# Feed-forward cut into 12 segments of 384 tokens, u stationary in its second layer, and one buffer each for raw q/k, v and shifts

## The chip, the cores and the metric

The kernel runs on one core of a Trainium2 chip. The metric is the device time of one execution in microseconds (us). Of the kernel before, three runs took 761.41, 757.99 and 758.09 us, so the median is 758.09 us. The engines are named as in the profile: PE is TensorE (the matrix engine; PEld is its weight loading), DVE is VectorE, ACT is ScalarE, POOL is GpSimd, and SP is the engine whose queue issues all the DMAs of this kernel.

## The reference

Eight sequences of 576 tokens go through causal attention with 8 heads of 64 and a bias from running sums, and then through a gated feed-forward of width 1024 with a convolution of three taps along the tokens.

```python
B, H, S, D = 8, 8, 576, 64
cum = np.cumsum(np.maximum(s, 0.0), axis=-1)
scores = np.matmul(q, k.transpose(0, 1, 3, 2)) / np.sqrt(D)
scores = scores + np.minimum(-(cum[..., :, None] - cum[..., None, :]), 0.0)
attn = softmax(np.where(causal, -1e9, scores))
x = np.matmul(attn, v).transpose(0, 2, 1, 3).reshape(B, S, 512)
h = np.maximum(x @ w_in, 0.0)                    # w_in: 512 x 1024
conv = sum(conv_w[k] * hp[:, k:k + S] for k in range(3))   # hp: h with a zero row at both ends
out = (h * sigmoid(conv)) @ w_out                # w_out: 1024 x 512, out: 8 x 576 x 512
```

## The kernel before, in words

**Work.** Two heads make a pair, four pairs a sequence, and there are 32 pairs. A pair's attention on PE is: shift products `sh` (scores whose maxima DVE takes, L1098 and L1130), a transpose of the maxima (L1156), the scores `sc` in 4 parts (L1209), column sums (L1324) and the product with v (L1267). ACT turns scores into weights (L1224). From pair 8 on, `ORDER` ties `sh` of the next pair, `sc` of this one and the sums and the product of the one before into one block on PE, which this text calls a burst.

**Feed-forward.** Each sequence is cut into two halves of 288 tokens. Half `hf` of sequence `b` runs its first layer once per 128 of the 1024 hidden channels (`moe_h`): 12 matmuls on a 290-column tile of x (288 and a neighbour at each side; 4 blocks of 128 inputs, times 3 products of high and low parts), then ReLU (L1437), the centre tap (L1442), two side taps (L1455), the sigmoid (L1467), the product with h (L1473), and the split of the result into a high part (L1481) and a low part (L1485), two channel blocks at a time. The second layer (`moe_o`, L1513) keeps a 128 by 128 block of w_out in the array and streams 288 columns of u past it; its result has the output channels on the partitions, so the kernel stores `outT` and the host transposes it. There are 1536 matmuls of 290 columns and 1536 of 288.

**What sets the order.** Every piece is a task of a planner (`Sched.play`), which walks forward with assumed durations and gives each engine the ready task with the smallest due number (`DUE`). The recorded order is then the program. The planner also holds the pools of buffers: a task that allocates waits until a slot is free. `BUFS` gives 2 raw q/k tiles, 2 tiles of q and k parts, 3 `ek`, 3 `eq` (the shifts), 5 u tiles and 2 output tiles; v has 2, and x has 5 and 7 tiles for the two halves. Until 112 us of its own plan the planner fills waits of PE with dummy matmuls (L1560).

Of the kernel before, what the change touches and what calls it, by code (L numbers as in the profile page):

```python
# [1628 lines left out]
```

## Time and profile before

| | before |
|---|---|
| median of three runs | 758.09 us |
| span of the profiled execution | 757.9 us |
| PE busy | 739.8 us, 98% |
| DVE, ACT, POOL busy | 490.4, 458.0, 381.5 us |
| matmuls of the feed-forward | 1536 of 290 columns, 1536 of 288 |
| last matmul ends, last ACT copy starts | 754.79, 754.85 us |

The profiled execution's span of 757.9 us stands 0.2 us below the median of the runs, so a sum made on the span is carried over by adding 0.2. A busy PE isn't PE at its peak: matmuls overlap, and a row's mean duration is longer than the distance from one matmul to the next. For the distance, the starts of a timeline or the pieces of the chain of waits are read.

### The profile page before, as it was taken

Reading aid. Unit: us, or ns where it says so; the run is one execution under the profiler, and the core shown is the slowest. Engines: PE = TensorE matmul, PEld = TensorE weight load, DVE = VectorE, ACT = ScalarE, POOL = GpSimd, SP = SyncE. Lnnn points to the kernel's source line nnn. Section 1 sums busy time; section 2 is a strip of 40 time slices with the busy share of each in tenths; the row PEclk is TensorE's granted clock in tenths of the full one; section 3 lists DMA queues with packets and bytes.
Section 4 is the critical chain, followed back from the end, with each engine's and each line's share of the span. In section 5 each row is a group of like instructions: output and inputs, shape, how many; then the busy total and the mean of one; then the engine's idle time right before and its main releaser. Section 6 shows DMA issues by size and latency. Waiting matters only on the chain.

```text
span 757.9 us, 20341 instructions
## 1 busy us (share of the span) xinstructions
PE 739.8 (98%) x7822; PEld 664.0 (88%) x7822; DVE 490.4 (65%) x1390; ACT 458.0 (60%) x1070; POOL 381.5 (50%) x459
## 2 busy tenths in 40 slices
PE   9999999999999999999999999999999999999998
PEld 7666779978989989898999899898998889899998
DVE  8676997545766657586664776666675866633632
ACT  5467887445765656555755756566575556653633
POOL 5257456524866444654755755654545446521211
PEclk9999999999999999999999999999999999999999
DMA  7877662223333231424333242333324131111000
GB/s 213 261 230 211 222 215 66 91 83 115 108 114 108 81 119 58 122 91 117 99 89 116 77 130 68 116 111 116 100 52 147 55 95 33 36 34 48 16 32 32
DMA packets 55159, 80.18 MB, mean 106 GB/s; under 512 B 14041, under 2 KB 34841, under 8 KB 55001
## 3 DMA queue, kind: packets, MB, share of 16 engines
q1 hardware_dynamic: 55061, 78.87, 33.9%
q8 instruction: 61, 1.00, 0.6%
q14 instruction: 37, 0.30, 0.1%
HBM read 67.48 MB, written 10.98 MB: 104 GB/s over the span
## 4 chain that ended last, share of the span: by engine, by line
PE 87%; DMA 5%; DVE 4%; issue 2%; ACT 1%; SPq 0%; POOL 0%; DVEq 0%; ACTq 0%
PE ps L1424 27%; PE ps L1513 27%; PE ps L1209 13%; PE pv L1267 11%; PE ps L1098 4%; PE ps L1324 3%; DVE ps L1130 2%; DMA bb<-cum_d 2%; DMA w<-w_in 1%; DMA eq<-rt 1%; DVE r L1130 1%; DMA rb<-ri_d 1%; DMA ri_d<-ri 1%; DMA v<-vp 0%; PE ps L1156 0%
## 5 line engine op out<-in xcount | busy, mean ns | idle before, releaser
L1513 PE MATMUL ps<-u,wo 128*128 128x288 f32 x1536 | 220.5, 298 | 0.9 <-ACT ob L1530 0.5
L1424 PE MATMUL ps<-x,wi 128*128 128x290 f32 x1536 | 218.8, 298 | 1.2 <-ACT ob L1530 1.2
L1424 PEld LDWEIGHTS ps<-x,wi 128*128 128x128 f32 x1536 | 209.8, 190 | 2.8 <-ACT ob L1530 1.4
L1513 PEld LDWEIGHTS ps<-u,wo 128*128 128x128 f32 x1536 | 207.2, 188 | 4.3 <-ACT ob L1530 0.7
L1224 ACT ACTIVATE pt<-ps,bias_sb 128x288 f32<-128x288 f32 (+4 forms) x384 | 155.2, 478 | 74.5 <-PE ps L1209 73.2
L1455 DVE SCALAR_TENSOR_TENSOR ct<-ps,cw_sb,ct 128x287 f32<-128x287 f32 (+1 forms) x256 | 129.2, 513 | 73.0 <-ACT ct L1442 70.7
L1485 POOL TENSOR_TENSOR u<-ct,u 128x576 fp32r<-128x576 f32 x64 | 92.0, 1439 | 161.4 <-ACT u L1481 123.5
L1130 DVE CUSTOM_DVE_ANT_0 ps<-ps,bb 128x64 f32<-128x64 f32 (+4 forms) x320 | 133.7, 452 | 53.8 <-PE ps L1098 27.4
L1209 PE MATMUL ps<-s 64*128 64x288 f32 (+4 forms) x1152 | 119.8, 306 | 5.8 <-DVE r L1130 4.5
L1209 PEld LDWEIGHTS ps<-s 64*128 64x128 f32 x1152 | 95.6, 185 | 16.8 <-DVE r L1130 11.5
L1071 POOL TENSOR_SCALAR_AFFINE_SELECT bb<-bb 128x256 f32<-128x256 f32 (+1 forms) x125 | 53.2, 433 | 105.8 <-DVE r L1130 86.6
L1242 POOL TENSOR_SCALAR_AFFINE_SELECT pt<-pt 128x256 f32<-128x256 f32 (+1 forms) x160 | 69.4, 445 | 65.5 <-ACT pt L1224 55.5
L1267 PE MATMUL pv<-pt,v 128*32 128x448 f32 (+4 forms) x1536 | 94.5, 389 | 2.3 <-DVE rb L1374 2.3
L1437 ACT ACTIVATE ps<-ps 128x289 f32<-128x289 f32 x128 | 50.8, 396 | 71.2 <-PE ps L1424 68.9
L1032 POOL TENSOR_TENSOR s<-raw,s 128x1152 fp32r<-128x1152 f32 x30 | 88.2, 2940 | 9.6 <-ACT s L1028 6.8
L1267 PEld LDWEIGHTS pv<-pt,v 128*32 128x32 f32 x1536 | 57.7, 110 | 35.4 <-issue 25.7
L1467 ACT ACTIVATE ct<-ct 128x288 f32<-128x288 f32 x128 | 56.2, 440 | 33.1 <-DVE ct L1455 32.6
L1473 DVE TENSOR_TENSOR ct<-ct,ps 128x288 f32<-128x288 f32 x128 | 57.1, 448 | 22.3 <-ACT ct L1467 21.2
L1442 ACT ACTIVATE ct<-ps,cw_sb 128x288 f32<-128x288 f32 x128 | 63.8, 498 | 5.3 <-ACT ps L1437 0.4
L1209 PE MATMUL ps<-eq,ek 64*128 64x288 f32 (+4 forms) x384 | 64.5, 300 | 1.2 <-DMA eq<-rt 1.2
L1098 PE MATMUL ps<-s 64*128 64x288 f32 (+4 forms) x384 | 58.7, 340 | 0.4 <-DVE r L1130 0.2
L1130 DVE DVE_READ_ACCUMULATOR2_ANT r<- 128x1 f32 x384 | 53.8, 140 | 0.0
(89 smaller groups left out, 687.8 us busy)
## 6 DMA issues: line engine op xcount, KB each, us to landing
raw<-qk SPq DMA_DIRECT2D x32, 576.0 KB
bb<-cum_d SPq DMA_DIRECT2D x32, 576.0 KB
v<-vp SPq DMA_DIRECT2D x32, 320.0 KB
rb<-ri_d SPq DMA_DIRECT2D x64, 144.0 KB
outT<-ob SPq DMA_DIRECT2D x64, 144.0 KB
w<-w_out SPq DMA_DIRECT2D x8, 512.0 KB
w<-w_in SPq DMA_DIRECT2D x8, 512.0 KB
rows_d<-bx SPq DMA_DIRECT2D x1, 1215.0 KB
```

The source lines that it names most:

```text
L1032: tt_on(e)(st[:, 0:2, :], R_t[raw.slot], st[:, 2:4, :].bitcast(F32), op=ALU.subtract)
L1098: nc.tensor.matmul(dst[j], l, S_t[sb.slot][r, 2, c0:c1], start=True, stop=not (early and diagonal(tau, c1)),)
L1130: nc.vector.tensor_tensor_reduce(out=src, in0=src, in1=in1, scale=1.0, scalar=acc if c0 else -3.0e38, op0=ALU.add, op1=ALU.max, accum_out=acc,
L1209: nc.tensor.matmul(dst[j], l, m, start=(k == 0), stop=(k == 3))
L1224: nc.scalar.activation(PT_t[pts[j].slot][0:jt, O_T[t] + c0 : O_T[t] + c1], bank(pb, o, o + c1 - c0)[0:jt], AF.Sigmoid, bias=bias_sb[0:jt, ...
L1242: nc.gpsimd.affine_select(out=reg, in_=reg, pattern=[[0, 2], [1, min(P, W_T[t])]], compare_op=ALU.is_ge, fill=0.0, base=0, channel_multipl ...
L1267: nc.tensor.matmul(pvt[gs, o0 : o0 + c1 - c0], vt[0:jt, t, gs], PT_t[pts[g // 2].slot][0:jt, O_T[t] + c0 : O_T[t] + c1], start=(t == 0), s ...
L1424: nc.tensor.matmul(bank(hb, 0, XW), l, r, start=(k == 0), stop=(k == len(seq) - 1))
L1442: nc.scalar.activation(C_t[ct.slot][:, i, :], bank(hb, 2 * hf, 2 * hf + HS), AF.Copy, scale=cw_sb[:, 3 * f + 1 : 3 * f + 2],)
L1455: nc.vector.scalar_tensor_tensor(cc[:, lo:hi], bank(hb, hf + sh + lo, hf + sh + hi), cw_sb[:, 3 * f + k : 3 * f + k + 1], cc[:, lo:hi], op ...
L1485: tt_on(e)(uu[:, 1], C_t[ct.slot], uu[:, 0].bitcast(F32), op=ALU.subtract)
L1513: nc.tensor.matmul(bank(pb, 0, HS), l, r, start=(fp == 0 and k == 0), stop=(fp == NF // 2 - 1 and k == len(seq) - 1),)
```

## The change

The tokens of two sequences in a row (1152) are cut into 3 segments of 384, the middle one made of the last 192 tokens of one and the first 192 of the next (each with its own neighbours: 2 times 194 columns). The first layer streams 386 or 388 columns. The second layer keeps a 128-token block of u in the array and streams 512 columns of w_out, so its result has the tokens on the partitions and the rows go out as the output has them. x is copied in two pieces per pair (`rb` gets a zero column at both ends). The first two parts of `sh` are cut at 448 and 576 columns instead of 288 and 576. raw, v and eq have one buffer each, and a second one for pairs 1, 3 and 5 (v: 1 and 3) that is given back before the u tiles are opened; `ek` has 2. The table `DUE` has new numbers.

```diff
-BUFS = 2, 2, 3, 3, 4, 5, 3, 2
+BUFS = 1, 2, 2, 1, 4, 5, 3, 2
-NX = (5, 7)
+NX = 11
+    SEG = 3 * P
+    CUT = S - SEG
+    PER = 2 * S // SEG
+    NSEG = B * S // SEG
+    FIRST = {"raw": (1, 3, 5), "v": (1, 3), "eq": (1, 3, 5)}
...
-    SH_PARTS = [[(L, 0, HS)], [(L, HS, S)], [(3, 0, P * 4 - PAD), (0, 0, P - PAD)],
+    SH_PARTS = [[(L, 0, S - P)], [(L, S - P, S)], [(3, 0, P * 4 - PAD), (0, 0, P - PAD)],
...
+        if b % 2 == 0:
+            pieces = [(seg, 0, 0, SEG + 2), (seg + 1, 0, SEG, CUT + 2)]
+        else:
+            pieces = [(seg + 1, CUT + 2, 0, CUT + 2), (seg + 2, 0, CUT, SEG + 2)]
...
-    def moe_h(b, hf, fp):
+    def moe_h(g, fp):
+        G = 2 if g % PER == 1 else 1
+        W = SEG // G
...
                     nc.tensor.matmul(
-                        bank(hb, 0, XW), l, r, start=(k == 0), stop=(k == len(seq) - 1)
+                        bank(hb, 0, G * (W + 2)), l, r, start=(k == 0), stop=(k == len(seq) - 1)
                     )
...
-                    seq += [(wo[:, 0, f, ms], uu[:, 0, i]), (wo[:, 1, f, ms], uu[:, 0, i]),
-                            (wo[:, 0, f, ms], uu[:, 1, i])]
+                    seq += [(uu[:, 0, i, ms], wo[:, 0, f, :]), (uu[:, 0, i, ms], wo[:, 1, f, :]),
+                            (uu[:, 1, i, ms], wo[:, 0, f, :])]
                 for k, (l, r) in enumerate(seq):
                     nc.tensor.matmul(
-                        bank(pb, 0, HS), l, r, start=(fp == 0 and k == 0),
+                        bank(pb, 0, DM), l, r, start=(fp == 0 and k == 0),
...
-                out[b, ms, hf * HS : (hf + 1) * HS], moe_tiles["ob"][ob.slot]
+                out.rearrange("b s d -> (b s) d")[r0 : r0 + P, :], moe_tiles["ob"][ob.slot]
```

On PE, behind the attention of the last pair, the program before has 14 groups of 6 matmuls of the second layer (two output tiles and most of two more) and then the first layer of the last half; these are its rows from the last product with v on:

```order
L1267 MATMUL pv<-pt,v_94 32x64 x4
L1513 MATMUL ps_65<-u_1744,wo 128x288 x6
L1513 MATMUL ps_65<-u_1743,wo 128x288 x6
L1513 MATMUL ps_65<-u_1745,wo 128x288 x6
L1513 MATMUL ps_65<-u_1741,wo 128x288 x6
L1513 MATMUL ps_66<-u_1744,wo 128x288 x6
```

The program now has, at the same place, 10 groups of 512 columns with w_out and u in each other's role, and behind them the first layer of segment 10:

```order
L1372 MATMUL pv<-pt,v_90 32x64 x4
L1622 MATMUL ps_65<-wo,u_1776 128x512 x6
L1622 MATMUL ps_65<-wo,u_1780 128x512 x6
L1622 MATMUL ps_65<-wo,u_1777 128x512 x6
L1622 MATMUL ps_65<-wo,u_1778 128x512 x6
L1622 MATMUL ps_66<-wo,u_1776 128x512 x6
L1622 MATMUL ps_66<-wo,u_1780 128x512 x6
L1622 MATMUL ps_66<-wo,u_1777 128x512 x6
L1622 MATMUL ps_66<-wo,u_1778 128x512 x6
L1622 MATMUL ps_65<-wo,u_1776 128x512 x6
L1622 MATMUL ps_65<-wo,u_1780 128x512 x6
L1541 MATMUL ps_66<-x,wi 128x388 x12
```

Over the whole program 256 such groups of 6 became 144, and 128 first-layer groups of 12 became 96 (64 of 386 columns, 32 of 388).

On SP, in the middle of the program, one round of a pair's DMAs before reads as follows; `eq` is the shift tile, `raw` the q and k of a later pair, and `rc`, `ri_d` and `rb` the way of the column sums:

```order
L1172 DMA eq_88<-rt_101 2x5x128
L1538 DMA outT<-ob_1746 128x288
L1346 DMA rc<-rs 64x1x9 x2
L1021 DMA v_95<-vp 128x640
L1356 DMA ri_d<-ri 128x9
L1366 DMA rb<-ri_d 64x576
L1366 DMA rb<-ri_d 64x4x144
L1042 DMA ek_85<-rows_d 9x576 x2
L1060 DMA bb_92<-cum_d 128x2x576
L1172 DMA eq_88<-rt_101 2x5x128
```

The same round in the program now is:

```order
L1277 DMA eq_86<-rt_96 2x5x128
L1110 DMA raw_81<-qk 128x1152
L1451 DMA rc<-rs 64x1x9 x2
L1117 DMA v_90<-vp 128x640
L1461 DMA ri_d<-ri 128x9
L1471 DMA rb<-ri_d 64x576
L1471 DMA rb<-ri_d 64x4x144
L1145 DMA ek_84<-rows_d 9x576 x2
L1110 DMA raw_81<-qk 128x1152
L1163 DMA bb_88<-cum_d 128x2x576
L1277 DMA eq_86<-rt_96 2x5x128
```

Before, 25 of the last 26 shift DMAs already went to the one tile `eq_88`; raw went to `raw_81` 14 times and to `raw_82` 12 times in the last 26. In the short gap between two bursts that comes before the product with v of pair 11, PE now has five groups of the second layer and the transpose of the maxima as the second row:

```order
L1622 MATMUL ps_65<-wo,u_1777 128x512 x6
L1261 MATMUL ps_66<-ident,r_94 128x128
L1622 MATMUL ps_65<-wo,u_1776 128x512 x6
L1622 MATMUL ps_65<-wo,u_1778 128x512 x6
L1622 MATMUL ps_65<-wo,u_1779 128x512 x6
L1622 MATMUL ps_69<-wo,u_1779 128x512 x6
L1203 MATMUL ps_65<-s_83 128x448
```

Before, the gap in front of pair 14's product has eight groups of the second layer (48 matmuls) and one of the first, and the transpose as the fourth row; the rows there are:

```order
L1513 MATMUL ps_67<-u_1741,wo 128x288 x6
L1513 MATMUL ps_67<-u_1744,wo 128x288 x6
L1424 MATMUL ps_68<-x,wi 128x290 x12
L1156 MATMUL ps_65<-ident,r_99 128x128
L1513 MATMUL ps_67<-u_1745,wo 128x288 x6
L1513 MATMUL ps_66<-u_1741,wo 128x288 x6
L1513 MATMUL ps_66<-u_1744,wo 128x288 x6
L1513 MATMUL ps_66<-u_1745,wo 128x288 x6
L1513 MATMUL ps_66<-u_1743,wo 128x288 x6
L1513 MATMUL ps_67<-u_1743,wo 128x288 x6
L1098 MATMUL ps_65<-s_83 128x288
```

Behind the last first-layer groups of segment 10 there stand four groups of the second layer and one of the first before a group that reads the u they lead to; in segment 11, the last one, six groups of the second layer stand there. The dummy matmuls of the start number 195 before and 217 now; all of them stand ahead of the first row of the feed-forward in both programs, and so do the products with v of pairs 0 to 4.

## Rows read from the trace of the kernel before

**Rows 1.** The page: busy time and share of each engine, and the granted clock in 40 slices.

```profile
PE 739.8 (98%) x7822; PEld 664.0 (88%) x7822; DVE 490.4 (65%) x1390; ACT 458.0 (60%) x1070; POOL 381.5 (50%) x459
...
PEclk9999999999999999999999999999999999999999
```

**Rows 2.** The chain of waits of the whole program: share of the span by line.

```profile
by line: PE ps L1424 27.4%; PE ps L1513 27.2%; PE ps L1209 13.2%; PE pv L1267 10.6%; PE ps L1098 4.2%; PE ps L1324 3.4%; DVE ps L1130 2.1%; issue 1.8%; DMA bb<-cum_d 1.5%; DMA w<-w_in 1.4%; DMA eq<-rt 0.7%; DVE r L1130 0.6%; DMA rb<-ri_d 0.
```

**Rows 3.** Busy time in two stretches: length, then each engine, clock, DMA share, GB/s.

```profile
0.00:101.00 101.00, 93.88 (x1164) 68.11 (x1168) 79.17 (x246) 67.71 (x144) 53.63 (x77) 1.00 0.76 231
166.00:687.00 521.00, 513.97 (x5479) 472.18 (x5481) 341.18 (x976) 317.10 (x757) 280.91 (x336) 1.00 0.30 92
```

**Rows 4.** Pieces of the chain at the end: start us, us, line, matmuls.

```profile
701.20 9.69 PE ps L1424 x72
...
742.08 12.71 PE ps L1513 x96
```

**Rows 5.** Timeline of PE in a burst: start us, us, line, tiles, shape, count.

```profile
316.85 0.56 PE L1209 MATMUL ps<-s 64*128 64x288 f32 x6
317.25 0.29 PE L1209 MATMUL ps<-eq,ek 64*128 64x288 f32 x2
317.38 0.39 PE L1098 MATMUL ps<-s 64*128 64x448 f32 x4
...
318.80 0.77 PE L1209 MATMUL ps<-s 64*128 64x448 f32 x6
319.40 0.37 PE L1209 MATMUL ps<-eq,ek 64*128 64x448 f32 x2
319.61 0.42 PE L1209 MATMUL ps<-s 64*128 64x64 f32 x6
...
320.29 0.62 PE L1209 MATMUL ps<-s 64*128 64x320 f32 x6
320.75 0.31 PE L1209 MATMUL ps<-eq,ek 64*128 64x320 f32 x2
320.89 0.47 PE L1209 MATMUL ps<-s 64*128 64x192 f32 x6
```

**Rows 6.** Timeline of PE at the start: dummy matmuls.

```profile
10.76 6.28 PE L1560 MATMUL pv<-still 64*128 64x256 bf16 x56
```

**Rows 7.** Waits of PE: line <- releaser: us in total, times, longest.

```profile
PE ps L1424 <- ACT ob L1530: 1.2, 1, 1.2
PE ps L1209 <- DMA eq<-rt: 1.2, 1, 1.2
```

**Rows 8.** Timeline of PE: the first matmuls behind one burst.

```profile
304.48 1.73 PE L1513 MATMUL ps<-u,wo 128*128 128x288 f32 x11
```

**Rows 9.** Timeline of the SP queue around the same place.

```profile
299.87 0.34 SPq L1021 DMA_DIRECT2D v<-vp  x1
...
308.91 0.61 SPq L1172 DMA_DIRECT2D eq<-rt  x1
309.97 0.36 SPq L1016 DMA_DIRECT2D raw<-qk  x1
```

**Rows 10.** Timeline of POOL: the low part of q and k.

```profile
307.28 2.66 POOL L1032 TENSOR_TENSOR s<-raw,s 128x1152 fp32r<-128x1152 f32 x1
```

**Rows 11.** Pieces of the chain in the first 120 us.

```profile
84.90 2.90 PE pv L1267 x48
...
98.48 2.83 PE pv L1267 x48
101.32 5.04 PE ps L1424 x36
```

**Rows 12.** Timeline of ACT at the end: ReLU of the last channels, last copy.

```profile
742.11 0.40 ACT L1437 ACTIVATE ps<-ps 128x289 f32<-128x289 f32 x1 [0.29 <-PE ps L1424]
...
754.85 0.40 ACT L1530 COPY ob<-ps 128x288 f32<-128x288 f32 x1 [0.40 <-PE ps L1513]
```

**Rows 13.** Timeline of POOL at the end: the last low part of u.

```profile
746.61 1.43 POOL L1485 TENSOR_TENSOR u<-ct,u 128x576 fp32r<-128x576 f32 x1 [1.93 <-ACT u L1481]
```

More of the change, by code (lines that the diff above doesn't have):

```diff
@@ L506, in play @@
                     lock[e] = needs
-                post(now + max(dur - HIDE[e], min(dur, 0.05)), "free", t)
+                hide = o[4] if len(o) > 4 else HIDE[e]
+                post(now + max(dur - hide, min(dur, 0.05)), "free", t)
                 if e == "SP":
@@ L613 @@
     base_sb = const.tile([2 * NT, NP, 2], F32, name="base_sb")
-    V_t = [const.tile([P, NT, P], F32, name=f"v{i}") for i in range(2)]
+    V_t = [const.tile([P, NT, P], F32, name="v0")]
     PT_a = const.tile([P, NPT, O_T[-1] + W_T[-1]], F32, name="pt")
     PT_t = [PT_a[:, i, :] for i in range(NPT)]
-    X_t = const.tile([P, sum(NX), 2, XW], F32R, name="x")
-    rb_t = const.tile([P, S], F32, name="rb")
+    X_t = const.tile([P, NX, 2, XW], F32R, name="x")
+    rb_t = const.tile([P, S + 2], F32, name="rb")
     R8_t = [const.tile([P, P], F32, name=f"r{i}") for i in range(2)]
@@ L623 @@
     rc_t, ri_t = (const.tile([P, RW], F32, name=n) for n in ("rc", "ri"))
-    H_a = const.tile([P, NHT, 2 * XW], F32, name="ht")
-    H_t = [H_a[:, i, :].rearrange("p (a c) -> p a c", a=2) for i in range(NHT)]
-    C_t = [const.tile([P, 2, HS], F32, name=f"ct{i}") for i in range(NHT)]
+    H_a = const.tile([P, NHT, S - P], F32, name="ht")
+    H_t = [H_a[:, i, :] for i in range(NHT)]
+    C_t = [const.tile([P, 2, SEG], F32, name=f"ct{i}") for i in range(NHT)]
     WPC = 256
@@ L655, in open_moe @@
         stage_stack.close()
+        early_stack.close()
         mp = ctx.enter_context(tc.tile_pool(name="mp", bufs=1))
-        moe_tiles["u"] = [mp.tile([P, 2, 2, HS], F32R, name=f"u{i}") for i in range(NRING)]
-        moe_tiles["ob"] = [mp.tile([P, HS], F32, name=f"ob{i}") for i in range(NOB)]
+        moe_tiles["u"] = [mp.tile([P, 2, 2, SEG], F32R, name=f"u{i}") for i in range(NRING)]
+        moe_tiles["ob"] = [mp.tile([P, DM], F32, name=f"ob{i}") for i in range(NOB)]
     sch = Sched()
@@ L675, in buf, with first, place @@
         return Buf(pools[name], n)
+    def first(name, p):
+        return buf(name + "_e" if p in FIRST[name] else name)
+    def place(b):
+        return 1 if b.pool in (pools["raw_e"], pools["v_e"], pools["eq_e"]) else b.slot
     def psb():
@@ L749 @@
     t_s = add("s", [("SP", 0.4)], [], -200, lambda e: nc.sync.dma_start(s_sb, s), nbytes=147456)
-    t_masks = add("masks", [("POOL", 4.4)], [], -190, c_masks)
+    t_masks = add("masks", [("POOL", 4.4, True)], [], -190, c_masks)
     t_pads = [
-        add(f"pads{i}", [("DVE", 2.0) if i == 0 else ("POOL", 2.2)], [], -189 + i,
+        add(f"pads{i}", [("DVE", 2.0) if i == 0 else ("POOL", 2.1, True)], [], -189 + i,
             c_pads(i))
@@ L755 @@
     ]
-    t_ident = add("ident", [("POOL", 2.9)], [], -189.5, c_ident)
+    t_ident = add("ident", [("POOL", 2.8, True)], [], -189.5, c_ident)
     t_ind = [
-        add(f"ind{i}", [("ACT", 0.72)], [t_masks], -187 + i, c_ind(EQ_t[i])) for i in range(NEQ)
+        add(f"ind{i}", [("ACT", 0.72)], [t_masks], -187 + i, c_ind(EQ_t[i])) for i in range(len(EQ_t))
     ]
@@ L767, in cum_chain @@
         )
-    t_cum8 = add("cum", [("DVE", 2.0, True)], [t_s, t_ones], -170, cum_chain)
+    t_cum8 = add("cum", [("DVE", 2.1, True)], [t_s, t_ones], -170, cum_chain)
     def grid_chain(e):
@@ L778, in grid_chain @@
         nc.vector.memset(ncr[:, 0:1], 0.0)
-    t_cum = add("grid", [("DVE", 1.5, True)], [t_cum8], -169, grid_chain)
+    t_cum = add("grid", [("DVE", 1.9, True)], [t_cum8], -169, grid_chain)
     def base_in(e):
@@ L1027, in hi @@
             st = S_t[sb.slot]
-            copy_on(e)(st[:, 2:4, :], R_t[raw.slot])
+            copy_on(e)(st[:, 2:4, :], R_t[place(raw)])
         def lo(e):
             st = S_t[sb.slot]
-            tt_on(e)(st[:, 0:2, :], R_t[raw.slot], st[:, 2:4, :].bitcast(F32), op=ALU.subtract)
+            tt_on(e)(st[:, 0:2, :], R_t[place(raw)], st[:, 2:4, :].bitcast(F32), op=ALU.subtract)
+        if p in FIRST["raw"]:
+            early_left.append(f"lo{p}")
+        if p in FIRST["v"]:
+            early_left.append(f"pv{p}")
+        if p in FIRST["eq"]:
+            early_left.append(f"sc{p}.{len(SC_PARTS) - 1}")
         t_hi = add(f"hi{p}", [("ACT", c_act(2 * S)), ("DVE", c_cp(2 * S), True, 2.0)], [t_load],
                    a_sh - HIA, hi, alloc=[sb], uses=[raw])
-        t_lo = add(f"lo{p}", [("POOL", c_pool(2 * S), True), ("DVE", c_tt(2 * S), True, 4.0 if p >= B0 else LO1)],
+        in_order("hi", t_hi)
+        t_lo = add(f"lo{p}", [("POOL", c_pool(2 * S) + 0.08, True), ("DVE", c_tt(2 * S), True, 4.0 if p >= B0 else LO1)],
                    [t_hi], A - LOA, lo, uses=[raw, sb])
@@ L1147, in pair @@
                         f"mx{p}.{j}.{tau}.{c0}",
-                        [("DVE", 0.19 + w / 0.96e3)],
+                        [("DVE", 0.235 + (c1 - c0) / 0.96e3, False, 0.0, 0.16 if c0 == 0 else 0.1)],
                         need, a_sh + 0.1 * i, sh_max, uses=[pbs[j], r8, bb],
@@ L1461, in moe_h @@
             for k in (0, 2):
-                t_k = add(f"ta{b}.{hf}.{f}.{k}", [("DVE", 0.53)], [t_k], tg + 0.1,
+                t_k = add(f"ta{g}.{f}.{k}", [("DVE", 0.63)], [t_k], tg + 0.1,
                           lambda e, k=k, tap=tap: tap(e, k), uses=[hb, ct])
@@ L1467, in gate @@
                 nc.scalar.activation(cc, cc, AF.Sigmoid)
-            t_g = add(f"ga{b}.{hf}.{f}", [("ACT", c_act(HS))], [t_k], tg + 0.2, gate, uses=[ct])
+            t_g = add(f"ga{g}.{f}", [("ACT", c_act(SEG))], [t_k], tg + 0.2, gate, uses=[ct])
             def mul(e, i=i, hb=hb):
-                cc = C_t[ct.slot][:, i, :]
-                nc.vector.tensor_tensor(cc, cc, bank(hb, 2 * hf, 2 * hf + HS), op=ALU.mult)
-            products.append(add(f"mu{b}.{hf}.{f}", [("DVE", c_tt(HS))], [t_g], tg + 0.2, mul,
+                nc.vector.tensor_tensor(mid(i), mid(i), seen(hb, 1), op=ALU.mult)
+            products.append(add(f"mu{g}.{f}", [("DVE", c_tt(SEG))], [t_g], tg + 0.2, mul,
                                 uses=[hb, ct]))
-        tg = h_tag(b, hf, 2 * fp + 1) + 0.2
+        tg = h_tag(g, 2 * fp + 1) + 0.2
         def u_hi(e):
@@ L1485, in u_lo, with moe_o @@
             tt_on(e)(uu[:, 1], C_t[ct.slot], uu[:, 0].bitcast(F32), op=ALU.subtract)
-        t_uh = add(f"uh{b}.{hf}.{fp}",
-                   [("DVE", c_cp(2 * HS), True, 1.0), ("ACT", c_act(2 * HS))],
-                   products + ([*t_wi.values(), *t_wo.values()] if b == 0 else []), tg, u_hi,
+        t_uh = add(f"uh{g}.{fp}",
+                   [("DVE", c_cp(2 * SEG), True, 1.0), ("ACT", c_act(2 * SEG))],
+                   products + ([*t_wi.values(), *t_wo.values(), *early_done] if g == 0 else []), tg, u_hi,
                    uses=[ct, u])
-        gate_done[b, hf, fp] = add(
-            f"ul{b}.{hf}.{fp}",
-            [("POOL", c_pool(2 * HS), True), ("DVE", c_tt(2 * HS), True, 3.0)], [t_uh], tg, u_lo,
+        gate_done[g, fp] = add(
+            f"ul{g}.{fp}",
+            [("POOL", c_pool(2 * SEG), True), ("DVE", c_tt(2 * SEG), True, 3.0)], [t_uh], tg, u_lo,
             uses=[ct, u],
         )
-        u_bufs[b, hf, fp] = u
-    def moe_o(b, hf, m):
+        u_bufs[g, fp] = u
+    def moe_o(g, m):
         ob, pb = buf("ob"), psb()
-        last = (b, hf) == (B - 1, 1)
-        tg = h_tag(b, hf, NF) + HT / NF * (1.0 + OTF * m)
+        last = g == NSEG - 1
+        tg = h_tag(g, NF) + HT / NF * (1.0 + OTF * m)
         ms = slice(m * P, (m + 1) * P)
@@ L1549 @@
             sch.need(d, sch.tasks[i])
-    for b in range(B):
-        for hf in range(2):
-            for fp in range(NF // 2):
-                moe_h(b, hf, fp)
-        for hf in range(2):
-            for m in range(NM):
-                moe_o(b, hf, m)
+    early_done = [t for t in sch.tasks if t.name in early_left]
+    for g in range(NSEG):
+        for fp in range(NF // 2):
+            moe_h(g, fp)
+        for m in range(SEG // P):
+            moe_o(g, m)
     def stay_awake(slot, mode, lane):
@@ L1627 @@
     r = _run(nc, [arrays], core_ids=[0])
-    return _np.ascontiguousarray(r.results[0]["outT"].transpose(0, 2, 1))
+    return _np.ascontiguousarray(r.results[0]["out"])
```

145 lines of the change are left out of this document (78 added, 67 removed), and 540 rows, old and new, of the table DUE.

## The prediction

> **What bounds the kernel now.** The page comes first: PE is busy for 739.8 of 757.9 us, no other engine for more than 65%, and its granted clock stays in the top tenth in every slice, that is at the 2.4 GHz level [rows 1]. So only what PE does, or waits for, can move the time. The chain of waits says of what this time is made: the two layers of the feed-forward hold 27.4 and 27.2% of the span, together 54.6% of 757.9, which is 413.8 us [rows 2]. Then the stretches: in the first 101 us, before the feed-forward begins, PE's busy time has dummies in it and DMA stands at 0.76 of its capacity; from 166 to 687 us PE is busy for 513.97 of 521 us, with DVE at 341 and ACT at 317 [rows 3]. In that long stretch an engine other than PE has a third of its time to spare.
>
> **The matmuls of the feed-forward.** The columns stay the same to the last one: 1536 times 290 is 768 times 386 plus 384 times 388, and 1536 times 288 is 864 times 512. What goes is 1056 of 3072 matmuls. So the gain is whatever a matmul costs beside its columns. Before, 72 matmuls of 290 columns take 9.69 us and 96 of 288 take 12.71 us, which is 134.6 and 132.4 ns each [rows 4]; in all 206.7 + 203.4 = 410.1 us. The trace has no full-height matmul of 386 or 512 columns. The nearest rows are the scores, where two matmuls of half height run side by side. Eight of them (four side-by-side steps) with 288 columns take from 316.85 to 317.38, 132.5 ns a step, just as the full-height ones; with 320 columns from 320.29 to 320.89, 150 ns; with 448 from 318.80 to 319.61, 202.5 ns [rows 5]. From 288 to 448 that is 0.4375 ns a column, from 320 to 448 it is 0.41. I take the middle, 0.425, since 448 is the row nearest to 512. Then 386 columns cost 134.6 + 96 x 0.425 = 175.4 ns, 388 cost 176.2, and 512 cost 132.4 + 224 x 0.425 = 227.6. The sum is 134.7 + 67.7 + 196.6 = 399.0 us, 11.1 less than now. The ends: with 0.41 the gain is 15.6 us; if all of a matmul's time went with its columns it is nothing.
>
> A rule speaks against this term. The rows show 132.4 ns for 288 columns, 12.4 ns above 288 columns at 2.4 GHz (120.0). The Trainium skill (TensorE: Matmul & The Clock Gate, section "Back-to-back issue gap") gives the gap as N/2.4 ns plus only 2.5 ns for a warm matmul; the trace doesn't agree with the sum of the two, as it has about 10 ns more, and if those 10 ns go with the columns, then 1056 matmuls give back only 2.6 us. That is the first rival below.
>
> **Edges.** The chain has 413.8 us for the two layers, the dense matmuls make 410.1. The 3.7 us between them are lost where one group ends and something else begins, over 384 groups; 240 are left, so 1.4 us go (0 to 3.7).
>
> **Dummies and the start.** One dummy takes 6.28 / 56 us, 0.112 us [rows 6], and 22 more stand before the first layer's first row: 2.5 us if each is a wait that PE wouldn't have had. They only fill waits and none is on the way of data, the weights and the first pairs' DMAs are the same ones in nearly the same order, and one `ek` tile less is cleared. So the bounds are -1 and +2.5, and I take +1.2.
>
> **Output tiles.** One wait of 1.2 us on a copy of the output [rows 7] should go: with two output tiles, PE came back to one after two times 24 matmuls of 132 ns (6.4 us), now after two times 24 of 228 ns (10.9 us). I take -1.2 (0 to -1.2).
>
> **One buffer each.** I cost this at nothing. Shifts: the DMA into `eq` is issued at 308.91, 4.4 us after the burst that reads the tile ended at 304.48 [rows 8, 9], and 25 of the last 26 pairs already use one and the same tile. It waits for the maxima, not for a buffer; of PE's waits only one of 1.2 us is for that DMA [rows 7]. v: its DMA is issued at 299.87, inside the burst [rows 9], as soon as the product with the old v is over, and is used in the next burst, some 14 us later. Raw: its DMA is issued at 309.97, right at the end of the low part of q and k at 307.28 + 2.66 = 309.94 [rows 9, 10]; so it waits for that operation already. With one tile the next load always waits so; behind it on SP stand only stores and the next pair's sums. If one of the three came late by 1 us a pair, 24 bursts would lose 24 us, but the shortest gap between bursts in which this has to fit is five groups, 30 x 0.228 = 6.8 us, where before it was eight groups of 132 ns matmuls, 6.4 us (at pair 30), and the waits of PE show none there.
>
> **Off the path.** x is copied in 64 pieces instead of 32, which costs ACT, DVE and POOL some 32 short operations each; the gate's operations get a third longer and a quarter fewer. All of it lies beside PE in the long stretch, in DVE's and ACT's spare third.
>
> **The end.** The last copy (0.40 us for 288 columns, at 754.85 [rows 12]) gets 512 columns, 0.6 us, and the last store 256 KB instead of 144. What lies behind the copy now is 757.9 - 755.25 = 2.65 us; I add 0.4 for it. Together +0.6 (0 to 2.3, if both went with their size).
>
> **The sum.** 757.9 - 11.1 - 1.4 + 1.2 - 1.2 + 0.6 = 746.0, and 0.2 for the median's distance from the profiled span: 746.2, or 746 us.
>
> **Rivals.**
>
> *The time goes with the columns.* For it: 10 of the 12.4 ns may be a slower stream, as the step from 288 to 448 gives 0.4375 ns a column, above the 0.4167 of 2.4 GHz. Against it: the step from 320 to 448 is 0.41. Then the first term is 0, and the time is 746.2 + 11.1 = 757.3; with the 0.4375 it is 7.3 us and the time 750, so this rival holds from 752 up. By the rule of the page named above it would be 754.7. Chance 0.16.
>
> *Fixed cost and the full clock.* The other end: slope 0.41, all edges gone: 746.2 - 4.5 - 2.3 = 739.4. Chance 0.12 for 736 to 742.
>
> *A starved start.* The second sequence's attention now has only segment 0 to be mixed with. Until the product with v of pair 8, 51 us of feed-forward were done before, and 35 us now; pairs 5 to 8 must follow each other faster by 16 us in all. Without any feed-forward the products of two pairs come 98.48 - 84.90 = 13.6 us apart [rows 11], while the weights are being unpacked. The attention of such a pair is some 11 us of PE, and the feed-forward in front of products 5 to 8 is 10.6, 4.2, 13.1 and 7.6 us: the tightest distance is 15.2 us, above 13.6. If the pairs can't go faster than the 25 us of before, up to 16 us come back: 750 to 762. Chance 0.07.
>
> *The gate is late (slower).* A segment's last hidden channels go through ReLU, taps, sigmoid, product and split before the second layer may use them. At the end of the kernel before, that way takes from 742.08, where the last first-layer matmul gives way [rows 4, 12], to 746.61 + 1.43 = 748.04 [rows 13]: 5.96 us. With 384 columns it is between 5.96 and 4/3 of it, 7.9 us. PE has in hand for it, by the order, 24 x 0.228 + 12 x 0.175 = 7.6 us in segment 10 and 36 x 0.228 = 8.2 in segment 11. If POOL or DVE make the way longer than 9 us, each of 12 segments waits over 1.3 us, and the kernel is slower than before; at 9.1 us it is 746 + 12 x 1.5 = 764. Chance 0.08.
>
> **How the numbers follow.** A measurement tells a change from none at about 0.5%, 3.8 us: faster is under 754.3, slower over 761.9. The forecast has 0.57, for 742 to 751, its own range. Faster is the forecast, the full clock, and half each of the starved start and a fifth of the first rival: 0.57 + 0.12 + 0.035 + 0.03, about 0.76. Slower is the gate, 0.08, with next to nothing from the starved start. The rest, 0.16, is no change. The range 739 to 757 leaves out some 0.05 below and 0.14 above.
>
> **What would show it.** In the profile after: second-layer matmuls 228 ns apart in the last stretch (235 would be the first rival, 225 the second), first-layer ones 175; the two layers at about 401 us in the chain; the first of them at 101 to 104 us; no wait of PE on the raw, v or eq DMAs; the product with v of pair 8 some 10 to 16 us earlier than now. A wait of PE on u, or on the gate's engines, in every segment would make me wrong.

## The result, and the profile after

The changed kernel takes 753.85 us, the median of 7 runs (752.56 to 754.83); the kernel before, beside it on the same chip, 760.89 (757.99 to 764.55). The ratio is 0.991, with a 95% interval of 0.988 to 0.994. So it is faster, but by about three fifths of what was forecast: the profiled spans went from 757.9 to 750.6 us, 7.3 less, where the sum of the terms was 11.9 less. 746 us was not reached, and 753.85 lies above the forecast's own range of 742 to 751.

The page and the head of the chain of waits of the kernel after, which answer to [rows 1, 2]:

```profile
PE 736.8 (98%) x6788; PEld 618.9 (82%) x6788; DVE 462.4 (62%) x1285; ACT 439.1 (59%) x975; POOL 390.3 (52%) x468
...
PEclk9999999999999999999999999999999999999999
...
by line: PE ps L1541 27.4%; PE ps L1622 27.3%; PE ps L1314 14.6%; PE pv L1372 10.7%; PE ps L1203 4.4%; PE ps L1429 3.3%; issue 1.3%; DVE ps L1235 1.2%; DMA w<-w_in 1.1%; ACT pt L1329 0.7%; PE ps L1669 0.6%; PE ps L1261 0.5%; ACT w L980 0.5%
```

PE is the bound as before, at the 2.4 GHz level in every slice. L1541 is the first layer, L1622 the second; together 54.7% of 750.6, which is 410.6 us. Before it was 413.8, and 401 was forecast. So the two layers gave 3 us in the chain, with a third of their matmuls gone. The costliest groups follow, first the kernel after, then before (busy us and the mean ns of one; a matmul's own time overlaps the next, so the means are not distances). Their busy time fell by 16 us, but a part of that is the overlap of each group's last matmul with what comes next, which is counted once for every group, and there are fewer groups:

```profile
L1622 PE MATMUL ps<-wo,u 128*128 128x512 f32 x864 | 211.7, 399 | 0.0
L1541 PE MATMUL ps<-x,wi 128*128 128x386 f32 (+1 forms) x1152 | 211.6, 340 | 0.1
```

```profile
L1513 PE MATMUL ps<-u,wo 128*128 128x288 f32 x1536 | 220.5, 298 | 0.9 <-ACT ob L1530 0.5 <-POOL u L1485 0.3
L1424 PE MATMUL ps<-x,wi 128*128 128x290 f32 x1536 | 218.8, 298 | 1.2 <-ACT ob L1530 1.2
```

Neither figure is the time gained. That is read from the distances, the time from the start of one matmul to the start of the next. The pace itself, in the last long pieces of the chain of the kernel after, the counterpart of [rows 4]:

```profile
676.57 12.77 PE ps L1541 x72
...
730.10 16.81 PE ps L1622 x72
```

16.81 / 72 is 233.5 ns for 512 columns, where 227.6 was forecast (and 235 named for the first rival); 12.77 / 72 is 177.4 for 386 and 388, where it was 176. From the start of every matmul to the next, leaving out those that come late at the edge of a group or behind a wait, the means are 134.5 and 132.4 ns before (1501 and 1463 distances) and 176.4 and 233.2 after (1115 and 813). By these the matmuls of the two layers, without edges and waits, went from 1536 x 134.5 + 1536 x 132.4 = 410.0 to 1152 x 176.4 + 864 x 233.2 = 404.7 us: 5.3 less, not 11.1. 1.9 came from the second layer, where 6.8 was expected, and 3.4 from the first, where it was 4.3.

All waits of PE in the kernel after (line <- releaser: us in total, times, longest):

```profile
PE ps L1669 <- DVE still L836: 3.9, 1, 3.9
PE ps L1314 <- ACT pt L1329: 2.6, 4, 1.2
PE ps L1669 <- DVE r L1235: 1.0, 2, 0.7
PE ps L1261 <- DVE r L1235: 0.5, 1, 0.5
PE ps L1669 <- ACT pt L1329: 0.4, 2, 0.3
PE ps L1261 <- DVE ct L990: 0.4, 1, 0.4
PE ps L1314 <- DVE r L1235: 0.2, 1, 0.2
```

There is no wait on raw, v or eq, none on u, none on the output tiles. The 3.9 us are the first dummy's, before any real work.

### The profile page after: what moved, and what is told of

Its sections match the earlier page's. It is cut to its first block, busy times and chain, and to the rows that moved or that the text cites. A ratio compares the mean times of both kernels' runs of the same rounds, so it can differ in the third digit from the quotient of the medians.

```text
span 750.6 us, 17949 instructions
## 1 busy us (share of the span) xinstructions
PE 736.8 (98%) x6788; PEld 618.9 (82%) x6788; DVE 462.4 (62%) x1285; ACT 439.1 (59%) x975; POOL 390.3 (52%) x468
## 4 chain that ended last, share of the span: by engine, by line
PE 89%; DVE 3%; ACT 2%; issue 1%; DMA 1%; SPq 0%; ACTq 0%; DVEq 0%
PE ps L1541 27%; PE ps L1622 27%; PE ps L1314 15%; PE pv L1372 11%; PE ps L1203 4%; PE ps L1429 3%; DVE ps L1235 1%; DMA w<-w_in 1%; ACT pt L1329 1%; PE ps L1669 1%; PE ps L1261 1%; ACT w L980 0%; DVE r L1235 0%; DVE w L990 0%; PE ps L1210 0%
## 5 line engine op out<-in xcount | busy, mean ns | idle before, releaser
L1622 PE MATMUL ps<-wo,u 128*128 128x512 f32 x864 | 211.7, 399 | 0.0
L1541 PE MATMUL ps<-x,wi 128*128 128x386 f32 (+1 forms) x1152 | 211.6, 340 | 0.1
L1541 PEld LDWEIGHTS ps<-x,wi 128*128 128x128 f32 x1152 | 202.5, 188 | 4.1 <-DVE r L1235 0.3
L1235 DVE CUSTOM_DVE_ANT_0 ps<-ps,bb 128x448 f32<-128x448 f32 (+3 forms) x320 | 143.7, 482 | 79.5 <-PE ps L1203 56.8
L1622 PEld LDWEIGHTS ps<-wo,u 128*128 128x128 f32 x864 | 159.6, 188 | 37.4 <-DVE r L1235 0.3
L1566 DVE SCALAR_TENSOR_TENSOR ct<-ps,cw_sb,ct 128x384 f32<-128x384 f32 x192 | 117.4, 615 | 72.5 <-ACT ct L1558 70.3
L1594 POOL TENSOR_TENSOR u<-ct,u 128x768 fp32r<-128x768 f32 x48 | 88.3, 1841 | 131.9 <-ACT u L1590 118.7
L1314 PE MATMUL ps<-s 64*128 64x288 f32 (+4 forms) x1152 | 125.4, 310 | 3.4 <-ACT pt L1329 2.6
L1314 PE MATMUL ps<-eq,ek 64*128 64x288 f32 (+1 forms) x348 | 63.9, 299 | 0.0
L1203 PE MATMUL ps<-s 64*128 64x448 f32 (+4 forms) x384 | 61.5, 343 | 0.3
L1558 ACT ACTIVATE ct<-ps,cw_sb 128x384 f32<-128x384 f32 x96 | 55.4, 577 | 2.6
```

The costliest lines, as they stand in the source:

```text
L1203: nc.tensor.matmul(dst[j], l, S_t[sb.slot][r, 2, c0:c1], start=True, stop=not (early and diagonal(tau, c1)),)
L1235: nc.vector.tensor_tensor_reduce(out=src, in0=src, in1=in1, scale=1.0, scalar=acc if c0 else -3.0e38, op0=ALU.add, op1=ALU.max, accum_out=acc,
L1314: nc.tensor.matmul(dst[j], l, m, start=(k == 0), stop=(k == 3))
L1541: nc.tensor.matmul(bank(hb, 0, G * (W + 2)), l, r, start=(k == 0), stop=(k == len(seq) - 1))
L1566: nc.vector.scalar_tensor_tensor(mid(i), seen(hb, k), cw_sb[:, 3 * f + k : 3 * f + k + 1], mid(i), op0=ALU.mult, op1=ALU.add,)
L1594: tt_on(e)(uu[:, 1], C_t[ct.slot], uu[:, 0].bitcast(F32), op=ALU.subtract)
```

## Experiments

To read the pace of a stream from a timeline row (start, us, count): the row lasts to the end of its last matmul, which alone is some 0.39 us at 512 columns, 0.34 at 386 and 0.30 at 288, so (us - 0.39) / (count - 1) is one distance at 512 columns. Since the start differs between profiles (below, e7), kernels that compute everything are compared from the first feed-forward matmul to the end of the last one: 653.5 us before (101.25 to 754.77), 644.7 after (102.23 to 746.89).

**e1: the pace by itself.** Three theories for 233 ns: columns, a fixed part, the neighbours.

```
for k in range(48):
    matmul(ps[:, 0:n], w[:, k % 8, :], x[:, 0:n])     # n = 288, 386, 512, ...
```

> The attention and the feed-forward are left out; TensorE alone runs series of 48 matmuls, each with its own weights: bf16 at 256 columns, then the kernel's fp32 form at 288, 386, 448, 512, 128, 192, 320 and 256 columns, bf16 at 288, 512 and 386, and at the end fp32 at 288, 512, 288 and 512 (24 each) beside copies and additions on VectorE, ScalarE and GpSimd. Read from start to start. Theory 'columns' (an fp32 column costs about 0.45 ns in a full-height matmul, by itself): 288 about 132 ns, 386 about 176, 512 about 233, alone and beside the other engines; bf16 at 512 about 216. Theory 'fixed part' (that of the prediction: some 10 ns a matmul and 0.425 ns a column): 288 132, 512 at most 228. Theory 'neighbours' (what the other engines do slows the stream in the kernel): alone 288 about 122.5 and 512 about 216, and 132 and 233 only in the last four series.

Timelines of PE, pieces of the series: fp32 with 288, 386 and 512 columns, bf16 with 512, and fp32 with 512 beside the other engines.

```profile
15.78 5.69 PE L44 MATMUL ps<-xr,wr 128*128 128x288 f32 x42
...
21.93 8.29 PE L44 MATMUL ps<-xr,wr 128*128 128x386 f32 x46
...
40.24 10.37 PE L44 MATMUL ps<-xr,wr 128*128 128x512 f32 x45
...
80.31 10.09 PE L44 MATMUL ps<-xb,wb 128*128 128x512 bf16 x46
...
111.69 4.03 PE L44 MATMUL ps<-xr,wr 128*128 128x512 f32 x17
```

That is 132, 177, 227, 216 and 227 ns. No theory has it whole. The neighbours do nothing. 288 and 386 columns cost here what they cost in the kernels. 512 costs 227, as the prediction had it, and 6 ns less than in the kernel. With bf16, 288 and 512 columns take 122.7 and 215.8 ns, and fp32 takes some 10 ns more at either width. The Trainium skill (TensorE: Matmul & The Clock Gate, "Back-to-back issue gap") gives N/2.4 + 2.5 ns as the gap of a warm matmul, which it calls that of an isolated one. The bf16 series of 48 agree with this formula, the fp32 ones don't.

**e2: what a switch costs.**

```
for k in range(8):
    run(512, 6)          # full height
    half(288, 2)         # then 32-column, bf16, or full-height work of 288 columns
```

> The attention and the feed-forward are left out; TensorE runs groups of 6 full-height matmuls of 512 columns, all data ready, with other work between the groups, 8 times each: two pairs of half-height matmuls, eight matmuls into 32 columns of the array, four bf16 matmuls, or six full-height ones of 288 columns; then half-height pairs alone at 288, 448 and 512 columns. Theory 'switch' (the array pays for the change from half-height or 32-column work to full height): the second matmul of a group starts about 95 ns later than the others (328 ns instead of 233) behind half-height and 32-column work, and not behind full-height work. Rival 'late data' (in the kernel that matmul waits for something that its neighbours write): no late second matmul anywhere here. For the pace of pairs: 'height' (half-height pairs are cheaper per column than full-height matmuls, which is what the prediction's slope hid) gives pairs of 512 at 228 ns or less each against 233 full; 'columns' gives the same 233.

Timeline of PE, and of its weight loads (PEld), around one piece of half-height work and the group behind it:

```profile
28.46 1.63 PE L44 MATMUL ps<-xr,wr 128*128 128x512 f32 x6
30.02 0.53 PE L54 MATMUL ps<-xr,wr 64*128 64x288 f32 x4
30.48 1.63 PE L44 MATMUL ps<-xr,wr 128*128 128x512 f32 x6
```

```profile
30.02 0.30 PEld L54 LDWEIGHTS ps<-xr,wr 64*128 64x128 f32 x4 [0.35 <-issue]
30.48 1.21 PEld L44 LDWEIGHTS ps<-xr,wr 128*128 128x128 f32 x6 [0.16 <-issue]
```

Six matmuls at 227 would make 5 x 0.227 + 0.39 = 1.53 us; it is 1.63. The group's first weights are loaded at 30.48, with its first matmul, not under the work before; the second matmul starts 333 ns after the first. The way back costs too: the last full-height matmul keeps 318 ns. The half-height work pays at both of its ends as well. From one group to the next it is 30.48 - 28.46 = 2.02 us, where six matmuls at 227 ns and two pairs at 131 (their pace in the series of pairs) make 1.62: about 0.4 us for the way there and back. Behind 32-column work the second matmul comes after 338 ns, behind full-height fp32 of 288 columns after 230. So "switch" holds. Behind bf16 the second comes after 314 ns, but the first had come 28 ns behind the last bf16 matmul, where these are 109 ns apart: 28 + 314 = 342 ns against 109 + 230, so next to nothing is lost there. Half-height pairs of 512 columns take 226 to 236 ns a pair: their pace is not another one, "height" falls.

**e3: halves.**

```
-    matmul(bank(pb, 0, DM), l, r, ...)
+    for c0 in (0, DM // 2):
+        matmul(bank(pb, c0, c0 + DM // 2), l, r[:, c0 : c0 + DM // 2], ...)
```

> The kernel after, with each second-layer matmul of 512 columns as two of 256 with the same weights: 1728 matmuls instead of 864, the same columns, the same order. Theory 'columns' (2.5 ns fixed and 0.448 a column): two take 234.4 ns for 233.2, +1.0 us, a profiled span of 751 to 753 us. Theory 'fixed part' (10 ns a matmul): +8.6 us, about 759 us. Should a second load of weights not fit beside 256 columns, more than that.

753.43 us, 0.987 of before (0.983 to 0.991); 642.0 us from the first to the last matmul. Both halves mark the start of a sum in the same bank, which changes the second layer's sums; e7 has that mended. The costliest group and the last piece of the chain:

```profile
L1623 PE MATMUL ps<-wo,u 128*128 128x256 f32 x1728 | 209.0, 280 | 0.0
```

```profile
731.34 16.35 PE ps L1623 x144
```

864 matmuls more, and the second layer is 2.7 us less busy: a distance is 114.9 ns, two are 229.8 against 233.2. Both theories had it longer. In this kernel it goes against the premise of the forecast, that what goes with a matmul comes back. In e1's stream the premise holds: 256 columns take 120 ns there, and two of them 240 against 227.

**e4: the old roles.**

```
-    seq += [(uu[:, 0, i, ms], wo[:, 0, f, :]), (uu[:, 0, i, ms], wo[:, 1, f, :]),
-            (uu[:, 1, i, ms], wo[:, 0, f, :])]
+    seq += [(wo[:, 0, f, ms], uu[:, 0, i]), (wo[:, 1, f, ms], uu[:, 0, i]),
+            (wo[:, 0, f, ms], uu[:, 1, i])]
```

> The kernel after, in segments of 384 tokens, but the second layer in its old roles: weights of the layer stationary, 384 columns of u moving, four blocks of channels, 1152 matmuls instead of 864 (the output is left as [channels, tokens], other than the reference's rows). Theory 'columns': 1152 x 174.5 = 201.0 us for the second layer against 864 x 233.2 = 201.5, a span of 750 to 752 us: the roles gave nothing, the segments all. Theory 'fixed part' with a 512-column matmul that is dear for a reason of its own in the new roles: 1152 x 175.4 = 202.1, span 751 to 753 - so the two differ in e1, not here. Rival 'roles' (u as stationary operand is slower, since its weights are fresh): the second layer falls to 1152 x 171 = 197 us and the span to about 746.

818.12 us, 1.071 of before (1.066 to 1.075). A fourth block per segment made the planner set another order, and PE now waits for its operands:

```profile
L1622 PE MATMUL ps<-u,wo 128*128 128x384 f32 x1152 | 222.2, 347 | 12.0 <-POOL u L1594 3.9
```

Nothing in the total speaks of the roles, and I didn't follow the loss. Only the pace is read: 173.3 ns for 384 columns.

**e6: the old roles in the same order.** Eight matmuls of 384 columns in e4's roles in the place of six of 512, every task where it was.

```
+    seq += seq[:2]
...
+    matmul(bank(pb, 0, SEG), l, r, ...)
```

> The kernel after, every task in its place, but with the second layer's six matmuls of 512 columns in a task replaced by eight of 384 with the layer's weights stationary and u moving (1152 instead of 864, the same columns in all; it computes sums other than the second layer's and stores 384 of the 512 columns). In e4 a 384-column matmul of that form took 173.3 ns, but the order of the tasks had changed with it. Theory 'roles count for little': 1152 x 173.3 = 199.6 us for the dense part against 864 x 233.2 = 201.5, so 1.9 us less: a span about 748.7 us. By the prediction's slope (0.425 ns a column and 11 fixed): 1152 x 175.4 = 202.1 against a 512-column matmul of 227.6, 196.7: the old roles would be 5.4 us worse than the new, a span of 756 us.

751.45 us, 0.988 of before (0.984 to 0.992); 643.0 us from the first to the last matmul against 644.7 after.

```profile
L1623 PE MATMUL ps<-u,wo 128*128 128x384 f32 x1152 | 210.0, 339 | 0.0
```

The dense distance is 173.3 ns again, 1152 of them 199.6 us. So 512 columns with u stationary brought nothing over 384 columns with u moving; it lost 1.7 us. What the change gained in matmul time it owes to the longer segments. This holds for the places of the operands as they are in these two kernels; e11 shows what the new roles cost at another place.

**e5: the operands.** Why 233 in the kernel and 227 in e1?

```
for k in range(48):
    matmul(ps, w[:, (0, 0, 1, 2, 2, 3)[k % 6], :], big[:, (0, 1, 0, 2, 3, 2)[k % 6], 0:512])
```

> The attention and the feed-forward are left out; TensorE alone runs series of 48 fp32 matmuls (one of 96). 512 columns: weights changing with one moving operand; weights and moving operand changing; the kernel's order (each weight block twice, then one once; two moving rows per channel block); the same weights all the time; moving operand or weights shifted by 4, 64 or 256 bytes. 256 columns in the kernel's order as halves, with changing weights, and with the same weights. 384, 386, 480 and 288 columns in the kernel's order. e1 had 227 for 512 with changing weights and one moving operand, the changed kernel has 233, and e3 has 114.9 for halves of 256, where e1 had 120. Theory 'operands' (which operands follow each other, or where they lie, sets the few ns above 512/2.4 = 213.3): the kernel's order gives 233 for 512 and 114 for the halves here too, the other series 227 and 120. Rival 'context' (the neighbours in the kernel set it): 227 and 120 in every series.

Two pieces of the timeline: the kernel's order, and changing weights with one moving operand that begins 4 bytes on:

```profile
36.25 10.85 PE L59 MATMUL ps<-big,wr 128*128 128x512 f32 x46
...
81.12 11.05 PE L59 MATMUL ps<-xr,wr 128*128 128x512 f32 x46
```

They give 232 and 237 ns. By the starts of the other series, one moving operand takes 226.7, weights from another place 232.4, halves in the kernel's order 118.4, not 114. So "operands" for 512 columns, with the neighbours out of it; the halves' pace it doesn't give. The moving rows lie 2080 bytes apart here and 2048 in the kernel, so this run can't tell the order of the operands from their place; e9 does.

**e9: the place.**

```
for s in range(0, 512, 16):           # 64 bytes a step
    second(u at U0 + s, w_out fixed)
```

> The attention and the feed-forward are left out; TensorE alone runs the second layer's order (512 columns, rows of 2048 bytes, 24 matmuls a series) with the stationary operand u moved by 64 bytes from one series to the next, 32 series; then the first layer's order with rows of x that begin 1552 bytes apart as in the kernel (388 columns), then 1568, 1584, 1600 and 1664, and with 386 and 384 columns. e5 had 226.7 to 236.6 ns for 512 columns by the operands alone. Theory 'place' (the distance of the two operands in memory sets the pace): the series differ by up to 6 ns and some places give 227; the kernel's own distance (the eighth series) 232 to 233; rows of x on multiples of 64 bytes are faster than 176. Rival 'order' (that the operands change at all): 231 to 233 at every place, and 176 at every pitch.

Timelines of PE in the first four series, and in the eighth, where the two operands lie as in the kernel:

```profile
16.71 5.04 PE L72 MATMUL ps<-wo__86,u__87 128*128 128x512 f32 x21
...
22.29 5.20 PE L72 MATMUL ps<-wo__86,u__87 128*128 128x512 f32 x22
...
27.79 5.16 PE L72 MATMUL ps<-wo__86,u__87 128*128 128x512 f32 x22
...
33.72 4.83 PE L72 MATMUL ps<-wo__86,u__87 128*128 128x512 f32 x20
...
55.15 5.53 PE L72 MATMUL ps<-wo__86,u__87 128*128 128x512 f32 x23
```

232, 229, 227, 234, and 234 ns. The four values repeat over all 32 series, that is every 256 bytes: 226.7 where u and w_out begin a multiple of 256 bytes apart, 233.5 at 64 bytes, 232.1 at 128, 228.9 at 192 (the first few matmuls of a series left out, and the places counted from the sizes of the tiles). By the same count the kernel's u lies 64 off, at the dearest of the four. In e5 it was the moving operand that was moved by 64 bytes, and the distance, stationary less moving, was 192: 228.9 ns there too. So it is the distance that counts, not the place of u alone. The rows of x, at 388 columns: 177 ns at 1552 bytes, 178 at 1568, 176 at 1584, 175 at 1600; but with 386 columns 175 at 1544 and 178 at 1600, so no simple rule shows here.

**e7: halves, mended.**

```
-    start=(fp == 0 and k == 0),
+    start=(fp == 0 and k == 0 and c0 == 0),
```

> The kernel after, with each second-layer matmul as two of 256 columns, and only the first half of a block marked as the start of its sum. Theory 'a 512-column matmul is dear here': the second layer takes 203.3 us as in e3, against 205.9 after; with the first feed-forward matmul at the same time as in the kernel after (102 us; it came at 105.6 in e3's profile) the span is 748 us, and the ratio to the kernel after 0.997. Rival 'lost again' (what the halves save is waited for elsewhere, or the later start belongs to them): the span is 751 us, as after.

752.15 us, 0.989 of before (0.986 to 0.993), and 642.3 us from the first to the last matmul, 2.4 less than after. Of that the span shows nothing, as the first feed-forward matmul comes at 104.9 us. The stretches of its profile, granted clock in the fifth column:

```profile
60.00:80.00 20.00, 19.26 (x259) 0.96 0.75 231
80.00:101.00 21.00, 20.12 (x280) 0.88 0.52 156
101.00:120.00 19.00, 18.92 (x199) 1.00 0.60 205
```

The clock fell to its lower level, 1.2 GHz, for part of 60 to 101 us, where dummies, weights and attention share PE and DMA. By these means that is 0.04 x 20 + 0.12 x 21 = 3.3 us of full-speed work lost; in the two profiles of the kernel after it stayed at 1.00. The halves come after that stretch. The profiles of e3, e6, e11 and e12 have the same fall (0.86 to 0.92 in 80 to 101 us) and their first feed-forward matmul at 104.4 to 105.6 us, so their spans can't be set beside the 750.6 of the kernel after; the time from the first to the last matmul can.

**e8: the kernel after again**, on the same chip as e6 and e7.

> The kernel after, unchanged, on the same chip as e6 and e7, so that they can be compared with it: 750 to 755 us, ratio to before 0.988 to 0.994; the first feed-forward matmul at 102 us if its place is the program's, anywhere from 102 to 106 if it is the chip's.

753.25 us, 0.991 of before (0.987 to 0.995); first feed-forward matmul at 102.4, 644.6 us from there. e6 and e7 are 1.8 and 1.1 us below it in the medians, less than these runs spread; in the traces they are 1.6 and 2.3.

**e10: a third output tile in the kernel before.**

```
-    moe_tiles["ob"] = [... for i in range(NOB)]
+    moe_tiles["ob"] = [... for i in range(NOB + 1)]     # used in turn
```

> The kernel before, every instruction in its place, but its output blocks go round three tiles instead of two, so that a copy never waits for the store of the block before the last. The prediction put 1.2 us of waits there. Theory 'tile' (the store holds the copy): PE's waits at L1513's successor for the output copy, 1.37 us at 591.8 and 0.65 at 725, go: about 2 us less, ratio to before 0.997. Rival 'queue' (the copy is late since ScalarE's queue stands behind a late key-sum on VectorE): they stay, ratio 1.000.

762.08 us, 1.001 of before (0.998 to 1.004). The waits of PE on the copy are still there:

```profile
PE ps L1425 <- ACT ob L1533: 1.2, 1, 1.2
...
PE ps L1516 <- ACT ob L1533: 0.5, 1, 0.5
```

So "tile" falls. Timelines of ACT and DVE in the kernel before show the queue at the first of the two waits, and, in the last row of ACT, the second:

```profile
591.09 0.68 ACT L1389 CAST x<-rb 128x580 fp32r<-128x580 f32 x1 [2.46 <-DVE rb L1374]
...
592.90 0.39 ACT L1530 COPY ob<-ps 128x288 f32<-128x288 f32 x1
...
725.34 0.40 ACT L1530 COPY ob<-ps 128x288 f32<-128x288 f32 x1 [0.85 <-PE ps L1513]
```

```profile
586.74 3.65 DVE L1290 TENSOR_TENSOR ht<-ht,pt 128x640 f32<-128x640 f32 x1 [2.32 <-POOL pt L1242]
590.31 0.74 DVE L1374 TENSOR_TENSOR rb<-pv,rb 128x576 f32<-128x576 f32 x1
```

A key sum of 3.65 us on DVE holds the next product, ACT stands 2.46 us before the cast that needs it, and the output copy stands behind that cast. [rows 7] had named the last link only. At 725 us it is not so: ACT had been idle for 0.85 us, waiting for PE's own result, when it began the copy. So "queue" holds for the longer wait, and neither theory for the shorter.

**e11: u moved by 192 bytes.**

```
+    mp.tile([P, 48], F32, name="u_place")
     moe_tiles["u"] = [mp.tile([P, 2, 2, SEG], F32R, ...) ...]
```

> The kernel after, every instruction in its place, with 192 unused bytes ahead of the u tiles, so that u and w_out begin a multiple of 256 bytes apart (they were 64 off). In e9 the second layer's order took 226.7 ns a matmul at that place and 233.5 at the kernel's. Theory 'place': 864 x (233.2 - 226.7) = 5.6 us less for the second layer, 200.3 us in place of 205.9, a span about 745 us and a ratio to before about 0.984. Rival 'neighbours' (inside the kernel groups of six never fall into the fast pace, as behind other work in e2): 229 to 231 ns, 2 to 3.6 us less, a ratio of 0.987. No change at all would say that place doesn't count in the kernel.

750.42 us (749.1 to 751.3), 0.984 of before (0.981 to 0.988): the lowest median of all. The kernel after wasn't run on this chip, so what the place gave is read from the traces. Its costliest group, and the last piece of its chain:

```profile
L1623 PE MATMUL ps<-wo,u 128*128 128x512 f32 x864 | 208.0, 395 | 0.0
```

```profile
729.10 16.38 PE ps L1623 x72
```

In the long stream at the end a matmul takes 16.38 / 72 = 227.5 ns; over all groups the mean is 228.8, for 233.2. The second layer is 3.7 us shorter, and from the first to the last matmul it is 641.1 us. So the place is a cause inside the kernel. Two thirds of the 5.6 us came, as the stream takes some ten matmuls to settle: over all its streams, the mean distances behind a switch go from 234 ns at the second matmul to 228 at the tenth and are 226 to 227 from the twelfth on; in the kernel after they stay near 233. Of the 51 streams 15 are only six matmuls long. At this place the new roles take 864 x 228.8 = 197.7 us, less than the 199.6 of e6, whose own place wasn't varied.

**e12: rows of x 1584 bytes apart.**

```
-    XW = SEG + 4
+    XW = SEG + 12
```

> The kernel after with one number changed: rows of x begin 1584 bytes apart instead of 1552, which also moves the u tiles behind them to a multiple of 256 bytes from w_out, as in e11. In e9 the first layer's order took 175.6 ns at this distance and 176.9 at the kernel's, at 388 columns. Theory 'place': the second layer as in e11 (5.6 us less) and the first 1152 x 1.0 to 1.3 = 1.2 to 1.5 us less, 205.3 us in place of 206.7: a span about 744 us, a ratio to before about 0.982. Rival 'neighbours': the second layer 2 to 3.6 us less and the first unchanged, a ratio of 0.987.

751.25 us, 0.986 of before (0.983 to 0.989). The second layer has 228.7 ns as in e11. The first has 177.3 where it had 176.4, and is 1.1 us more busy:

```profile
L1541 PE MATMUL ps<-x,wi 128*128 128x386 f32 (+1 forms) x1152 | 212.7, 341 | 0.1
```

The theory was wrong for x. A likely reason, not tested, is that the series of e9 used four of the eleven tiles of x, whose distances from the weights are not those of the others; its series of 386 columns had spoken against the theory already.

## Why the prediction was wrong, and where it was right

*Columns: the step that failed.* It said -11.1 us, and it was -5.3. Its premise, "the gain is whatever a matmul costs beside its columns", with 0.425 ns a column between 288 and 512, put 227.6 ns on the new second layer. A bare stream does run at 227 (e1), and from 288 to 512 columns it gains 0.42 ns a column, so the slope was right for a stream at that place; but in this kernel it is 233.2, 864 x 5.6 = 4.8 us more. e5 and e9 show where these come from: the distance in memory of the two operands, at which 512 columns go from 226.7 to 233.5; e11 took 3.7 of them back by moving u. The first layer was 0.7 ns dearer than forecast, 0.8 us. Why it is dearer is not known. The step that failed is thus above all the pace of the new second layer: the forecast took a time per column from half-height rows and carried it to operands at other places, as if the place didn't count. With the kernel's places 256 columns take 114.9 ns (e3), 288 132.4, 384 173.3 (e6), 386 176.4 and 512 233.2: 0.449 to 0.460 ns a column, so that hardly a fixed part was left to be saved. The term lies between the forecast's -11.1 and the first rival's nothing ("the time goes with the columns"); that rival's variant, the slope of 0.4375 with -7.3, was nearest. But this is no proof of a dearer column, as e1's stream shows.

*Edges.* -1.4 forecast. By the starts, before, 36 ends and 68 beginnings of groups keep PE some 90 to 96 ns longer, after 30 and 57: 9.8 and 8.2 us, -1.6. Right in size, but by luck: it was read as 3.7 us over 384 groups, of which 144 go, and is 9.8 us over 104 edges, of which 17 went. It goes with the number of switches between forms, as in e2, not of groups. 26 of the 68 beginnings, and 25 of the 57, stand behind the transpose of the maxima, which itself kept PE only some 28 ns before; with the 84 ns of the late matmul that makes 112 ns, near the 110.5 of a matmul of 128 columns in e1, so these are not lost.

*Output tile.* -1.2 forecast; two waits on the copy, 1.4 and 0.6 us by the starts, are gone, and one of 0.5 on u: 2.5 us in all. Not for the reason given: a third tile changes nothing (e10). ACT's queue held the copy in the longer wait, and after the change no copy stands behind such a cast at a bad moment. That the change removes these waits by its order and not by luck is not shown.

*Start.* +1.2 forecast: the first feed-forward matmul moved from 101.25 to 102.23, +1.0. Why was not tested; more than the dummies changed, as the first scores come at 15.14 us instead of 9.06. A term that the forecast lacked: behind the first feed-forward matmul the 26 transposes of the maxima (L1156, now L1261) keep PE for 1.4 us instead of 0.7, +0.7.

*End.* +0.6 forecast: from the last matmul's end to the span's it went from 3.1 to 3.7 us. Right.

*One buffer each.* Costed at nothing, and PE has no wait on raw, v or eq. The kernel after with two buffers each was not tried, so this rests on the waits alone.

*Starved start and late gate.* Neither came. Pair 8's product with v starts at 168.7 us for 186.1, 17 us earlier (10 to 16 forecast), and PE never waits for u.

The measured terms: -5.3 - 1.6 - 2.5 + 1.0 + 0.7 + 0.6 = -7.1, for 7.3 in the span.

## What to carry to other kernels

Fewer, wider matmuls save only what a stream of both widths shows in the same form, data type and place; measure that stream before counting on it. Count the switches between forms of matmul (half height, narrow columns, full height) as a cost of their own: about 0.4 us for the way there and back in e2. And when a fp32 stream is a few ns above its bare pace, look at where its two operands begin in memory: here a pad of 192 bytes gave 3.7 us, where the new roles without it lost 1.7.
